# Linformer attention into a maxout block: batch 0 with fewer TensorE instructions, and 120 small products ahead of everything

## The chip, the cores and the metric

The kernel runs on one core of one Trainium2 chip. The metric is device time in microseconds of one execution. Three executions of the kernel before took 319.89, 320.08 and 320.24 us; the median is 320.08 us. Engine names are those of the profile: PE is TensorE (PEld its weight loads), DVE is VectorE, ACT is ScalarE, POOL is GpSimd and SP is SyncE.

## The reference: what is computed

There are 8 batches of 8 heads, 1024 positions and 64 features per head. Keys and values are first projected along the sequence to 64 rows by two constant matrices E and F; then comes ordinary softmax attention; then a feed-forward block whose gate is the larger of two linear maps.

```python
k_proj = np.einsum('ks,bhsd->bhkd', E, k)          # 64 rows instead of 1024
v_proj = np.einsum('ks,bhsd->bhkd', F, v)
scores = scale * np.matmul(q, k_proj.transpose(0, 1, 3, 2))
attn = softmax(scores)                              # over the 64 projected keys
x = np.matmul(attn, v_proj)                         # heads side by side: (8192, 512)
out = np.maximum(x @ w1, x @ w2) @ w_out            # 512 -> 1024 -> 512
```

The inputs are float32 and so is the output; most products run in half precision, with sums in float32.

## The kernel before, in words

**Order.** The order of all instructions is written out by hand: each engine's queue gets its instructions in the order in which the Python code issues them. A long list of slots sets the order from batch 1 on; batch 0 is a straight list of calls (lines 955 to 1004), and it is the only part that the change touches. A "unit" is half of a batch's positions; from batch 1 on, the attention of one unit is woven between the feed-forward products of the unit before.

**Loads.** SP loads E, the first two heads of k (in float32, as `kf_sb`) and F. GpSimd's queue loads the rest with a cast to half precision, in this order: heads 2 and 3 of k, heads 0 to 3 of q, heads 4 to 7 of k, heads 4 to 7 of q (lines 116 to 118), the four pairs of heads of v (L108, called from line 123), then pieces of the weights w2 and w1 (L130, L139), then w_out and the later batches. A weight load is issued when one of eight earlier loads has landed.

**Batch 0.** `step_eft` (L167) transposes E, and later F, in float32 on PE, eight products of 64 columns each; DVE (for E) or ACT (for F) copies the result to half precision as `eft` (L173). `step_kv` (L195) projects k or v: for "k" it makes eight products of 64 output rows and 256 columns for four heads, and DVE copies the result to `kp` (L205). For "v" it works on two heads at a time and makes every product twice, once into the upper and once into the lower 64 rows of the bank (16 products of 128 columns per pair of heads), because the later steps want v in both halves. `step_kpt` (L285) transposes the projected keys, head by head and twice per head, again to have them in both halves of the partitions; DVE copies them to `kpt` (L290). `step_qt` (L311) transposes the queries; DVE copies them to `qt` (L316). `step_sc` (L340 through `score`) makes the scores of four heads and 256 positions: 32 keys at a time, so 16 products on array tiles of 64 rows by 32 columns; ACT takes the exp (L380). `step_dn` (L352) sums the exps by products with ones, on 64x32 tiles, and ACT takes the logarithm (L388); `step_inv` (L427) turns that into the inverse. `step_at` (L352) makes the values, and DVE scales them into `xt` (L443). Then the difference of the weights `wd` is formed by DVE (L540) and the up-projection starts (`up_slots`, L524).

**Dummies.** `warm(n)` (L153) issues n products of 128x512 ones whose result nobody reads. Eight stand in front of all; five, three, and several times two stand between the steps of batch 0.

**PSUM.** Four single banks go round in turn (`mm_bank`), and two double banks (`att_banks`). A step that takes a bank waits until the last reader of the step before it in that bank is done.

**Guard.** Near the end a flag decides whether a second, general version of the kernel (`tile_shifted`) has to run; here it does not. The last product (L1196) waits for a store, so that a fetch of instructions comes behind it.

Of the kernel before, what the change touches and what calls it, by code (L numbers as in the profile page):

```python
# [19 lines left out]
def kernel(  # L20
# [58 lines left out]
    def big(n, dtype=FP16):  # L79
        return const.tile([128, 16384 // mybir.dt.size(dtype) // 2], dtype, tag=f"big{n}", name=f"big{n}")  # L80
# [47 lines left out]
    for g in range(2):  # L128
        for w_sb, w in ((w2_sb, moe_w2), (w1_sb, moe_w1)):
            nc.gpsimd.dma_start(  # L130
                out=w_sb.rearrange("p (g z) f -> p g z f", z=2)[:, g, :, 0:256],
                in_=w.rearrange("(g p z) f -> p g z f", p=128, z=2)[:, g, :, 0:256],
            )
    for w_sb, w, f0, f1 in (
# [3 lines left out]
        for z in range(2):  # L138
            nc.gpsimd.dma_start(  # L139
                out=w_sb.rearrange("p (g z) f -> p g z f", z=2)[:, :, z, f0:f1],  # L140
                in_=w.rearrange("(g p z) f -> p g z f", p=128, z=2)[:, :, z, f0:f1],
# [3 lines left out]
    ones16 = const.tile([128, 512], FP16)  # L145
# [1 line left out]
    junk = const.tile([1, 1], FP16)  # L147


    def warm(n, att=False):  # L150
        w_ps = att_banks()[:, 0, :] if att else mm_bank()
        for _ in range(n):
            nc.tensor.matmul(  # L153
                out=w_ps, lhsT=ones16[:, 0:128], rhs=ones16, start=True, stop=True
            )

    warm(8)
    ident16 = const.tile([128, 128], FP16)
    nc.vector.tensor_copy(out=ident16, in_=ident)


    eft = [const.tile([128, NC, KP], FP16, tag=f"eft{i}", name=f"eft{i}") for i in range(2)]

    def step_eft(i):
        eft_ps = mm_bank()
        for c in range(NC):
            nc.tensor.transpose(  # L167
                out=eft_ps[:, c * KP : (c + 1) * KP],
                in_=ef_sb[:, i].rearrange("k (p c) -> k c p", c=NC)[:, c, :],
                identity=ident[:KP, :KP],  # L170
            )
        eng = nc.scalar.copy if i else nc.vector.tensor_copy
        eng(out=eft[i].rearrange("p c k -> p (c k)"), in_=eft_ps)  # L173


    def new_attn(t):
# [6 lines left out]
    def step_kv(t, h0=0, h1=H, which="kv", att=False, dma=False, copy=nc.vector.tensor_copy, between=None):  # L183
        kv_ps = att_banks()[:, 0, :] if att else mm_bank(n=0 if dma else None)
        n = (h1 - h0) * D
        both = which == "v"
        nh = 2 if both else h1 - h0
        for h in range(0, h1 - h0, nh):
            if h and between is not None:
                between()  # L190
            for c in range(NC):
                for w in which:
                    i = "kv".index(w)
                    for r in range(2) if both else (i,):
                        nc.tensor.matmul(  # L195
                            out=kv_ps[r * KP : (r + 1) * KP, h * D : (h + nh) * D],
                            lhsT=eft[i][:, c, :],
                            rhs=t[w][:, h0 + h : h0 + h + nh, c, :],
                            start=(c == 0), stop=(c == NC - 1),
                        )  # L200
        zd = lambda ap: ap.rearrange("p (h d z) -> p h z d", d=D // 2, z=2)
        if "k" in which:
            eng = nc.vector.tensor_copy if which == "k" or dma else nc.scalar.copy
            kp = t["kp"][:, h0:h1]
            eng(out=kp[:, :, 0, :], in_=kv_ps[0:KP, 0:n].rearrange("p (h d) -> p h d", d=D))  # L205
        if both:
            copy(out=t["vp"][:, h0:h1], in_=zd(kv_ps[:, 0:n]))
        elif "v" in which:
            def finish_v():
                nc.vector.tensor_copy(out=t["vp"][KP:128, h0:h1], in_=zd(kv_ps[KP:128, 0:n]))  # L210
                if dma:
                    nc.vector.tensor_copy(out=kp[:, :, 1, :], in_=kp[:, :, 0, :])
                    step_kpt_dma(t)
                else:
                    step_vp(t, h0, h1)

            if att:
                return finish_v
            finish_v()
# [47 lines left out]

    def kpt_of(t, head, o):
        rows = t["kpt"][o * D : (o + 1) * D]
        if "sets" not in t:  # L270
            return rows[:, head]
        s, m = divmod(head, H // 2)
        return rows[:, 2 * ORDER.index((m - o) % (H // 2)) + s]
# [6 lines left out]

    def step_kpt(t, h0=0, h1=H, att=False):
        kpt_ps = att_banks(FP16)[:, 0, :] if att else mm_bank(FP16)
        for h in range(h0, h1):
            for r in range(2):
                nc.tensor.transpose(  # L285
                    out=kpt_ps[r * D : (r + 1) * D, (h - h0) * KP : (h - h0 + 1) * KP],
                    in_=t["kp"][:, h, 0, :],
                    identity=ident16[:KP, :KP],
                )
        nc.vector.tensor_copy(  # L290
            out=t["kpt"][:, h0:h1, :].rearrange("q h k -> q (h k)"),
            in_=kpt_ps[:, 0 : (h1 - h0) * KP],
        )


    def step_kpt_dma(t):
        nc.sync.dma_start_transpose(
            out=t["kpt"], in_=t["kp"].rearrange("p h r d -> p (h r d)")
        )
# [6 lines left out]
    def step_qt(t, h0, nh=2, i0=0, i1=NI, att=False):  # L306
        qt_ps = att_banks(FP16)[:, 0, :] if att else mm_bank(FP16)
        ni = i1 - i0
        for h in range(nh):
            for i in range(ni):  # L310
                nc.tensor.transpose(  # L311
                    out=qt_ps[:, (h * ni + i) * 128 : (h * ni + i + 1) * 128],
                    in_=t["q"][:, h0 + h, 2 * (i0 + i) : 2 * (i0 + i) + 2, :],
                    identity=ident16,
                )
# [14 lines left out]
    W = HALF // 2  # L330
    Z = D // 2

    def score(t, g, j, banks):
        for h in range(2):
            for o in range(2):
                for e in range(2):
                    head = 4 * g + 2 * h + e
                    for s in range(2):
                        pos = D * (o ^ e) + s * Z
                        nc.tensor.matmul(  # L340
                            out=banks[e][pos : pos + Z, h * W : (h + 1) * W],
                            lhsT=kpt_of(t, head, o)[:, s * Z : (s + 1) * Z],
                            rhs=t["qt"][o * D : (o + 1) * D, head, j * W : (j + 1) * W],
                            start=True, stop=True,
                        )
        t["ex", g, j] = soft.tile([128, 2, HALF], FP16, tag="soft", name="ex_sb")
# [608 lines left out]
    t = tiles[0]  # L955
# [2 lines left out]
    step_eft(0)  # L958
    nc.vector.tensor_copy(out=t["k"][:, 0], in_=kf_sb[:, 0])
    nc.scalar.copy(out=t["k"][:, 1], in_=kf_sb[:, 1])  # L960
    warm(5)
    step_kv(t, 0, 4, "k")
    step_eft(1)
    step_kpt(t, 0, 4)
    warm(3)
    step_qt(t, 0, 4, 0, NI // 2)
    step_qt(t, 0, 4, NI // 2, NI)
    warm(2)
    step_sc(t, 0, 0)
    step_sc(t, 0, 1)  # L970
    warm(2)
    step_kv(t, 4, 8, "k")
    step_dn(t, 0, 0)
    warm(2)
    step_kpt(t, 4, 8)
    step_dn(t, 0, 1)
    step_inv(t, 0, 0)
    step_inv(t, 0, 1)
    warm(2)
    step_qt(t, 4, 4, 0, NI // 2)  # L980
    step_qt(t, 4, 4, NI // 2, NI)
    warm(2)
    step_sc(t, 1, 0)
    step_kv(t, 0, 2, "v")
    step_kv(t, 2, 4, "v")
# [95 lines left out]
    t = tiles[1]  # L1081
# [29 lines left out]
    t = tiles[2]  # L1111
# [8 lines left out]
    for b in range(3, B):  # L1120
        t = tiles[b]
        n = 2 * b - 3
# [13 lines left out]
    for i, (new, old) in enumerate(zip([*groups[1:], none], groups)):  # L1136
        n, h = divmod(i + 2, 2)
# [9 lines left out]
    for n, (b, o) in enumerate(units):  # L1147
# [44 lines left out]
    for reg in regs:  # L1192
# [4 lines left out]
        out=mm_bank()[0:1, 0:1], lhsT=ones16[:, 0:1], rhs=ones16[:, 0:1], start=True, stop=True  # L1197
# [166 lines left out]
```

## Time and profile before

| | |
|---|---|
| median of three executions | 320.08 us |
| span of the profiled execution, first to last instruction | 318.1 us |
| time of the profiled execution beside its span | not listed apart; the median is 2.0 us over the span |
| PE busy | 312.3 us, 98% |
| DVE, ACT, POOL busy | 76%, 65%, 13% |
| PE instructions recorded | 3922 weight loads and 3922 products |
| fetches of instructions on queue q8 | 31 packets, 0.51 MB |
| granted clock of PE | 1.000 over the span |

A line of the lists names the line of the code, the engine, the operation, output and inputs with the buffer numbers left out, shapes, count, and either busy time and mean or start and length; what stands in square brackets is the idle time before it and what ended it. A busy PE is not a PE at its peak, as the ends of products are modelled. In the DMA part, a queue's line gives packets, MB and the time of its packets as a share of the 16 engines' time. q0 holds GpSimd's loads, q1 those of SP and ACT, and q8 fetches instructions in packets of 16 KB.

### The profile page before, as it was taken

How to read it: one execution, taken by the hardware profiler on the slowest of the kernel's cores; microseconds unless marked ns; L12 is line 12 of the kernel's file. 1: busy time of each engine (PE TensorE's matmuls, PEld its weight loads, DVE VectorE, ACT ScalarE, POOL GpSimd, SP SyncE). 2: the span in 40 equal slices, each digit the busy share in tenths (PEclk: the TensorE clock that was granted, in tenths of full speed). 3: DMA queues.
4: the chain of work that ended last, by engine and by line, in shares of the span. 5: the costliest groups of instructions: out<-in, count | busy, mean ns of one | idle time of the engine just before them, and what ended most of it. 6: DMA issues, size and time to landing. Idle time of an engine off the chain costs nothing.

```text
span 318.1 us, 9308 instructions
## 1 busy us (share of the span) xinstructions
PE 312.3 (98%) x3922; PEld 253.6 (80%) x3922; DVE 241.1 (76%) x441; ACT 206.2 (65%) x373; POOL 40.8 (13%) x63
## 2 busy tenths in 40 slices
PE   8989999999999999999999999999999999999996
PEld 3555588888887888788887888788887888888885
DVE  2366888877969696996969696996969696969883
ACT  2476842777776777477776778477776777765541
POOL 8259002003000300022000400030000000000000
PEclk9999999999999999999999999999999999999999
DMA  7999999999979999899999999989979131313124
GB/s 189 206 200 195 207 206 202 207 158 160 204 139 195 162 212 245 210 182 154 223 233 217 167 204 245 215 151 183 232 149 209 45 102 36 102 35 102 36 99 136
DMA packets 76684, 53.71 MB, mean 169 GB/s; under 512 B 29664, under 2 KB 76128, under 8 KB 76640
## 3 DMA queue, kind: packets, MB, share of 16 engines
q0 software_dynamic: 30688, 28.05, 56.0%
q1 hardware_dynamic: 45664, 24.85, 32.7%
q8 instruction: 31, 0.51, 0.6%
q10 hardware_dynamic: 288, 0.20, 0.2%
q14 instruction: 13, 0.11, 0.1%
HBM read 57.15 MB, written 16.78 MB: 232 GB/s over the span
## 4 chain that ended last, share of the span: by engine, by line
PE 92%; DMA 5%; POOL 1%; ACT 1%; issue 0%; DVE 0%; POOLq 0%
PE mm_ps L837 47%; PE mm_ps L745 27%; PE mm_ps L524 4%; DMA v_sb<-in_v_dram 4%; PE att_ps L352 3%; PE mm_ps L195 3%; PE mm_ps L340 2%; PE mm_ps L633 2%; PE att_ps L237 1%; DMA out_dram<-o_sb 1%; PE mm_ps L311 1%; POOL k_sb L108 0%; POOL q_sb L108 0%; ACT ld_sb L388 0%; ACT ex_sb L380 0%
## 5 line engine op out<-in xcount | busy, mean ns | idle before, releaser
L719 ACT COPY p_sb<-mm_ps 128x512 f32<-128x512 f32 x179 | 101.8, 592 | 49.1 <-PE mm_ps L745 27.2
L837 PEld LDWEIGHTS <-big 128*128 128x128 f16 x768 | 73.5, 98 | 11.8 <-issue 3.6
L837 PE MATMUL mm_ps<-T_sb,big 128*128 128x256 f16 x576 | 76.9, 273 | 0.0
L760 DVE TENSOR_TENSOR gt_sb<-mm_ps,p_sb 128x512 f16<-128x512 f32 x56 | 38.5, 687 | 43.0 <-PE mm_ps L745 41.6
L745 PE MATMUL mm_ps<-big,big 128*128 128x256 f16 x336 | 50.4, 273 | 0.0
L745 PEld LDWEIGHTS <-big 128*128 128x128 f16 x448 | 43.8, 98 | 5.1
L837 PE MATMUL mm_ps<-wo_sb,gt_sb 128*128 128x256 f16 x256 | 42.6, 273 | 0.0
L837 PEld LDWEIGHTS <-gt_sb 128*128 128x128 f16 x376 | 35.7, 98 | 6.7 <-issue 2.7
L469 ACT ACTIVATE ex_sb<-mm_ps 128x512 f16<-128x512 f32 x50 | 27.2, 596 | 18.0 <-PE mm_ps L340 12.3
L745 PEld LDWEIGHTS <-wd_sb 128*128 128x128 f16 x336 | 32.9, 98 | 3.8
L745 PE MATMUL mm_ps<-xt_sb,wd_sb 128*128 128x256 f16 x224 | 32.8, 273 | 0.0
L499 DVE TENSOR_TENSOR xt_sb<-att_ps,ld_sb 128x1024 f16<-128x1024 f32 x26 | 31.7, 1219 | 0.2
L837 PE MATMUL mm_ps<-m_sb,xt_sb 128*128 128x256 f16 x128 | 24.4, 273 | 0.0
L303 POOL COPY junk<-qt_sb 1x1 f16<-1x1 f16 x6 | 2.1, 346 | 172.5 <-DMA qt_sb<-q_sb 172.5
L868 DVE TENSOR_TENSOR o_sb<-mm_ps,p_sb 128x512 f32<-128x512 f32 x32 | 21.9, 683 | 2.8 <-ACT p_sb L897 2.0
L763 DVE TENSOR_SCALAR gt_sb<-gt_sb 128x512 f16<-128x512 f16 (+1 forms) x60 | 20.9, 348 | 2.1
L705 DVE TENSOR_TENSOR big<-gt_sb 128x1024 f16<-128x1024 f16 x32 | 21.8, 683 | 0.0
L837 PE MATMUL mm_ps<-wo_sb,big 128*128 128x256 f16 x128 | 21.5, 273 | 0.0
L806 ACT ACTIVATE gt_sb<-mm_ps 128x512 f16<-128x512 f32 x28 | 16.8, 601 | 5.7 <-PE mm_ps L745 5.7
L837 PE MATMUL mm_ps<-T_sb,gt_sb 128*128 128x256 f16 x120 | 20.3, 273 | 0.0
L837 PEld LDWEIGHTS <-xt_sb 128*128 128x128 f16 x188 | 18.3, 98 | 2.3 <-issue 0.2
L760 DVE TENSOR_TENSOR gt_sb<-p_sb 128x512 f16<-128x512 f32 x28 | 19.1, 682 | 0.6 <-ACT p_sb L719 0.6
(121 smaller groups left out, 434.7 us busy)
## 6 DMA issues: line engine op xcount, KB each, us to landing
out_dram<-o_sb SPq DMA_DIRECT2D x62, 256.0 KB
k_sb<-in_k_dram POOLq DMA_DIRECT2D x7, 1024.0 KB, 9.8
v_sb<-in_v_dram POOLq DMA_DIRECT2D x7, 1024.0 KB, 15.3
q_sb<-in_q_dram POOLq DMA_DIRECT2D x5, 1024.0 KB, 23.0
q_sb<-in_q_dram POOLq DMA_DIRECT2D x6, 512.0 KB, 15.8
big<-in_moe_w_dram POOLq DMA_DIRECT2D x12, 128.0 KB, 6.3
v_sb<-in_v_dram POOLq DMA_DIRECT2D x4, 256.0 KB, 13.6
wo_sb<-in_moe_w_out_dram POOLq DMA_DIRECT2D x1, 1024.0 KB, 10.4
```

The lines of the kernel that those rows point to most:

```text
L195: nc.tensor.matmul(out=kv_ps[r * KP : (r + 1) * KP, h * D : (h + nh) * D], lhsT=eft[i][:, c, :], rhs=t[w][:, h0 + h : h0 + h + nh, c, :], ...
L469: nc.scalar.activation(out=t["ex", g, j][:, e, :], in_=banks[e], func=ACTF.Exp, scale=scale)
L499: nc.vector.tensor_tensor(out=x_out(t, g, j).rearrange("q z o n -> q o z n"), in0=at_ps.rearrange("q o (z n) -> q o z n", z=2), in1=ld[:, ...
L524: nc.tensor.matmul(out=h_ps, lhsT=wd_sb[:, r, fb * 128 : (fb + 1) * 128], rhs=t["xt"][:, r, :, j * W : (j + 1) * W], start=(r == 0), stop= ...
L705: nc.vector.tensor_tensor(out=S(i), in0=S(0) if x is None else x, in1=y(), op=op)
L719: copy(out=x, in_=bank)
L745: nc.tensor.matmul(out=bank[:, m * W : (m + 1) * W], lhsT=w_[:, n_, (2 * d + m) * 128 : (2 * d + m + 1) * 128], rhs=a[:, n_, :], start=(n ...
L760: nc.vector.tensor_tensor(out=c_blk(j, c), in0=two(x), in1=two(y), op=ALU.add)
L763: nc.vector.tensor_scalar_max(ap, ap, 0.0)
L806: nc.scalar.activation(out=out, in_=in_, func=ACTF.Relu)
L837: nc.tensor.matmul(out=bank[i][:, 0:CH] if two_banks else bank[:, i * CH : (i + 1) * CH], lhsT=a(c)[:, i * 128 : (i + 1) * 128], rhs=w_(c) ...
L868: nc.vector.tensor_tensor(out=o_sb, in0=two(x), in1=two(y), op=ALU.add)
```

## The change

All of it concerns batch 0 and the start.

- Ahead of everything stands `burst(120)`: 120 products of 64 rows by 32 output columns, 128 columns wide, whose places go round over eight tiles of the array. Behind it stand four dummies instead of eight.
- The dummies inside batch 0 become `warm32`: float32 products with the identity, in blocks of up to four times 128 columns. `warm32(5)` is two instructions, the others one.
- When F is transposed, ACT makes a second copy, `f_twice`, in which each block of F^T stands twice side by side (in the space of `big(3)`, which the transposed weights use later). The v projection of batch 0 uses it as a weight of 128 columns: one product where there were two.
- The keys of batch 0 are copied flat, with the first head repeated behind the last by a small ACT copy; `step_kpt` then transposes two neighbouring heads in one product: four per call instead of eight. `kpt_of` looks up the head accordingly.
- The scores of batch 0 use all 64 keys of a head at once: 8 products on 64x64 tiles instead of 16 on 64x32.

PE's program grows by 60 instructions in all: 240 come in front and 180 go from batch 0.

```diff
-    def warm(n, att=False):
-        w_ps = att_banks()[:, 0, :] if att else mm_bank()
+    def warm(n):
+        w_ps = mm_bank()
...
-    warm(8)
+    def warm32(n):
+        w_ps = mm_bank()
+        for i in range(0, n, 4):
+            m = min(4, n - i)
+            nc.tensor.matmul(
+                out=w_ps[:, 0 : m * 128], lhsT=ident,
+                rhs=ident[:, None, :].broadcast_to([128, m, 128]), start=True, stop=True,
+            )
+
+    def burst(n):
+        w_ps = att_banks()
+        for i in range(n):
+            a, z = divmod(i % 8, 4)
+            nc.tensor.matmul(
+                out=w_ps[32 * z : 32 * z + 32, a, 0:128],
+                lhsT=ones16[64 * a : 64 * a + 64, 0:32],
+                rhs=ones16[64 * a : 64 * a + 64, 0:128],
+                start=True, stop=True,
+            )
+
+    burst(120)
+    warm(4)
...
+    f_twice = big(3)[:, 0 : NC * 2 * KP].rearrange("p (c k) -> p c k", c=NC)
...
+        if i:
+            nc.scalar.copy(
+                out=f_twice.rearrange("p c (r k) -> p c r k", r=2),
+                in_=eft_ps.rearrange("p (c k) -> p c k", k=KP)[:, :, None, :].broadcast_to([128, NC, 2, KP]),
+            )
...
-                    for r in range(2) if both else (i,):
-                        nc.tensor.matmul(
-                            out=kv_ps[r * KP : (r + 1) * KP, h * D : (h + nh) * D],
-                            lhsT=eft[i][:, c, :],
...
+                    nc.tensor.matmul(
+                        out=kv_ps[:, h * D : (h + nh) * D] if both
+                        else kv_ps[i * KP : (i + 1) * KP, h * D : (h + nh) * D],
+                        lhsT=f_twice[:, c, :] if both else eft[i][:, c, :],
...
+            if which == "k":
+                flat = kp.rearrange("p h r d -> p (h r d)")
+                eng(out=flat[:, 0:n], in_=kv_ps[0:KP, 0:n])
+                nc.scalar.copy(out=flat[:, n : n + D], in_=kv_ps[0:KP, 0:D])
...
-        for h in range(h0, h1):
-            for r in range(2):
-                nc.tensor.transpose(
-                    out=kpt_ps[r * D : (r + 1) * D, (h - h0) * KP : (h - h0 + 1) * KP],
-                    in_=t["kp"][:, h, 0, :],
...
+        flat = t["kp"][:, h0:h1].rearrange("p h r d -> p (h r d)")
+        for h in range(h1 - h0):
+            nc.tensor.transpose(
+                out=kpt_ps[:, h * KP : (h + 1) * KP],
+                in_=flat[:, h * D : (h + 2) * D],
...
-                    for s in range(2):
-                        pos = D * (o ^ e) + s * Z
+                    z = D if t is tiles[0] else Z
+                    for s in range(0, D, z):
+                        pos = D * (o ^ e) + s
...
-    warm(5)
+    warm32(5)
```

The other calls of `warm` inside batch 0 become calls of `warm32` with the same argument.

More of the change, by code (lines that the diff above doesn't have):

```diff
@@ L193, in step_kv @@
                     i = "kv".index(w)
-                    for r in range(2) if both else (i,):
-                        nc.tensor.matmul(
-                            out=kv_ps[r * KP : (r + 1) * KP, h * D : (h + nh) * D],
-                            lhsT=eft[i][:, c, :],
-                            rhs=t[w][:, h0 + h : h0 + h + nh, c, :],
-                            start=(c == 0), stop=(c == NC - 1),
-                        )
+                    nc.tensor.matmul(
+                        out=kv_ps[:, h * D : (h + nh) * D] if both
+                        else kv_ps[i * KP : (i + 1) * KP, h * D : (h + nh) * D],
+                        lhsT=f_twice[:, c, :] if both else eft[i][:, c, :],
+                        rhs=t[w][:, h0 + h : h0 + h + nh, c, :],
+                        start=(c == 0), stop=(c == NC - 1),
+                    )
         zd = lambda ap: ap.rearrange("p (h d z) -> p h z d", d=D // 2, z=2)
@@ L204, in step_kv @@
             kp = t["kp"][:, h0:h1]
-            eng(out=kp[:, :, 0, :], in_=kv_ps[0:KP, 0:n].rearrange("p (h d) -> p h d", d=D))
+            if which == "k":
+                flat = kp.rearrange("p h r d -> p (h r d)")
+                eng(out=flat[:, 0:n], in_=kv_ps[0:KP, 0:n])
+                nc.scalar.copy(out=flat[:, n : n + D], in_=kv_ps[0:KP, 0:D])
+            else:
+                eng(out=kp[:, :, 0, :], in_=kv_ps[0:KP, 0:n].rearrange("p (h d) -> p h d", d=D))
         if both:
@@ L269, in kpt_of @@
         rows = t["kpt"][o * D : (o + 1) * D]
+        if t is tiles[0]:
+            n = H // 2
+            return rows[:, head // n * n + (head - o) % n]
         if "sets" not in t:
@@ L282, in step_kpt @@
         kpt_ps = att_banks(FP16)[:, 0, :] if att else mm_bank(FP16)
-        for h in range(h0, h1):
-            for r in range(2):
-                nc.tensor.transpose(
-                    out=kpt_ps[r * D : (r + 1) * D, (h - h0) * KP : (h - h0 + 1) * KP],
-                    in_=t["kp"][:, h, 0, :],
-                    identity=ident16[:KP, :KP],
-                )
+        flat = t["kp"][:, h0:h1].rearrange("p h r d -> p (h r d)")
[3 more added lines that the diff above has]
+                in_=flat[:, h * D : (h + 2) * D],
+                identity=ident16[:KP, :KP],
+            )
         nc.vector.tensor_copy(
@@ L337, in score @@
                     head = 4 * g + 2 * h + e
-                    for s in range(2):
-                        pos = D * (o ^ e) + s * Z
+                    z = D if t is tiles[0] else Z
+                    for s in range(0, D, z):
+                        pos = D * (o ^ e) + s
                         nc.tensor.matmul(
-                            out=banks[e][pos : pos + Z, h * W : (h + 1) * W],
-                            lhsT=kpt_of(t, head, o)[:, s * Z : (s + 1) * Z],
+                            out=banks[e][pos : pos + z, h * W : (h + 1) * W],
+                            lhsT=kpt_of(t, head, o)[:, s : s + z],
                             rhs=t["qt"][o * D : (o + 1) * D, head, j * W : (j + 1) * W],
@@ L964 @@
     step_kpt(t, 0, 4)
-    warm(3)
+    warm32(3)
     step_qt(t, 0, 4, 0, NI // 2)
     step_qt(t, 0, 4, NI // 2, NI)
-    warm(2)
+    warm32(2)
     step_sc(t, 0, 0)
     step_sc(t, 0, 1)
-    warm(2)
+    warm32(2)
     step_kv(t, 4, 8, "k")
     step_dn(t, 0, 0)
-    warm(2)
+    warm32(2)
     step_kpt(t, 4, 8)
@@ L978 @@
     step_inv(t, 0, 1)
-    warm(2)
+    warm32(2)
     step_qt(t, 4, 4, 0, NI // 2)
     step_qt(t, 4, 4, NI // 2, NI)
-    warm(2)
+    warm32(2)
     step_sc(t, 1, 0)
```

## The prediction

> **What bounds the kernel now.** I read the page first (busy time), then PE's waits, the chain of waits from 17 to 28 us, the time-ordered list of the first 32 us, and last the DMA queues in narrow stretches.
>
> ```profile
> span 318.1 us, 9308 instructions
> PE 312.3 (98%) x3922; PEld 253.6 (80%) x3922; DVE 241.1 (76%) x441; ACT 206.2 (65%) x373; POOL 40.8 (13%) x63
> ```
>
> The list of PE's waits over the whole span (total us, times, longest):
>
> ```profile
> PE mm_ps L195 <- DMA v_sb<-in_v_dram: 0.5, 2, 0.3
> PE att_ps L352 <- ACT vp_sb L207: 0.5, 1, 0.5
> ```
>
> TensorE is full from about 23 us to the end; its only waits inside the work lie in batch 0. The change touches nothing behind batch 0 on the path, so its time is the shift of the moment at which PE becomes continuous. The chain of waits there (start, length):
>
> ```profile
> 5.54 13.33 DMA v_sb<-in_v_dram
> ...
> 18.92 0.64 PE mm_ps L195 x16
> 19.56 0.28 PE att_ps L352 x8
> ...
> 19.86 0.60 ACT ld_sb L388
> 20.46 0.91 ACT ex_sb L380
> ...
> 22.39 0.33 ACT vp_sb L207
> ...
> 22.76 0.63 PE att_ps L352 x32
> 23.39 1.83 PE mm_ps L524 x8
> ```
>
> The second v pair lands at 18.88; then the sums (L352), then ScalarE without a pause from 19.86 to 22.72, then values, then the up-projection (L524). Beside it runs a VectorE chain and a load gate (list in order of time):
>
> ```profile
> 20.49 2.48 DVE L443 TENSOR_TENSOR xt_sb<-mm_ps,ld_sb 128x512 f16<-128x512 f32 x4 [0.60 <-ACT ld_sb L388]
> 22.89 0.48 DVE L540 TENSOR_TENSOR wd_sb<-big,big 128x256 f16<-128x256 f16 x2
> 27.02 0.69 DVE L540 TENSOR_TENSOR wd_sb<-big,big 128x1024 f16<-128x1024 f16 x1 [0.89 <-DMA big<-in_moe_w_dram]
> 27.77 3.13 PEld L524 LDWEIGHTS <-wd_sb 128*128 128x128 f16 x16 [0.42 <-DVE wd_sb L540]
> ```
>
> So two chains meet at 23.3 to 23.4 (ScalarE's, and VectorE's 20.49 + 2.48 + 0.48), and at 27.7 PE is held once more by a weight load through VectorE (27.02 + 0.69 = 27.71). A gain ahead of 27 us is worth only what this gate gives back too.
>
> Why v lands when it does. GpSimd issues each weight load on the landing of an earlier one, so its idle ends show landings; and a narrow stretch of the DMA queues shows the fetch of PE's instructions (q8: packets, MB, share):
>
> ```profile
> 13.11 0.70 POOL L130 DMA_DIRECT2D big<-in_moe_w_dram x1 [1.81 <-DMA k_sb<-in_k_dram]
> 15.65 0.71 POOL L130 DMA_DIRECT2D big<-in_moe_w_dram x1 [1.84 <-DMA q_sb<-in_q_dram]
> 18.27 0.70 POOL L139 DMA_DIRECT2D big<-in_moe_w_dram x1 [1.92 <-DMA v_sb<-in_v_dram]
> ```
>
> ```profile
> q8 instruction: 31, 0.51, 0.6%
> ```
>
> From 15.9 to 16.0 us, and from 22.9 to 23.0 us:
>
> ```profile
> q8 instruction: 1, 0.02, 59.1%
> q8 instruction: 1, 0.02, 58.4%
> ```
>
> 1 MB of q takes 15.65 - 13.11 = 2.54 us, so half of it, the first v pair, should take 1.27 us and end GpSimd's wait at 16.9; it ends at 18.27, 1.35 us late. In that stretch lies one 16 KB fetch of instructions. A fetch sits on one DMA engine and holds that engine's sixteenth of every load behind it. 7,844 recorded PE instructions over 31 fetches is one per 253. Counted in the code, the 256th instruction is the second key transpose (15.0 us), the 512th lies in the values L352 at 20 us: the fetches show 0.9 and about 3 us later.
>
> **The change, part by part.** PE in the front and ScalarE, from the same list:
>
> ```profile
> 1.47 3.59 PE L153 MATMUL mm_ps<-ones 128*128 128x512 f16 x8 [1.47 <-DVE ones L146]
> 4.99 1.09 PE L167 MATMUL mm_ps<-ident,big 64*128 64x64 f32 x8
> 6.02 1.25 PE L153 MATMUL mm_ps<-ones 128*128 128x512 f16 x5
> 7.29 1.06 PE L195 MATMUL mm_ps<-k_sb,eft 128*64 128x256 f16 x8
> 10.36 1.07 PE L311 MATMUL mm_ps<-ident,q_sb 128*128 128x128 f16 x16
> 17.34 0.41 PE L340 MATMUL att_ps<-qt_sb,kpt_sb 64*32 64x256 f16 x16
> 18.03 0.64 PE L195 MATMUL mm_ps<-v_sb,eft 128*64 128x128 f16 x16 [0.28 <-DMA v_sb<-in_v_dram]
> 19.61 0.40 PE L340 MATMUL att_ps<-qt_sb,kpt_sb 64*32 64x256 f16 x16
> ```
>
> ```profile
> 9.42 0.59 ACT L173 CAST eft<-mm_ps 128x512 f16<-128x512 f32 x1 [2.25 <-PE mm_ps L167]
> 12.27 1.94 ACT L380 ACTIVATE ex_sb<-att_ps 128x1024 f16<-128x1024 f32 x2 [2.27 <-PE att_ps L340]
> 17.82 1.02 ACT L380 ACTIVATE ex_sb<-att_ps 128x1024 f16<-128x1024 f32 x1 [0.57 <-PE att_ps L340]
> 25.71 1.01 ACT L562 COPY big<-att_ps 128x1024 f16<-128x1024 f16 x1 [2.47 <-PE att_ps L556]
> ```
>
> *Burst and four dummies for eight.* Eight dummies take 3.59 us, about 0.43 each, where five later ones take 1.25, 0.25 each: PE starts at half rate and is at full rate by 6 us. Four fewer give back 1.7 us. The burst spreads over eight array tiles, as the scores do. Sixteen score products of 256 columns take 0.41 with the pipeline's end; 120 of 128 columns at half rate are 7.5 such groups of equal time, at most 3.1 us, and 1.6 us if groups of eight follow each 0.107 us (half of the 256-column step, 0.43 / 2 / 2). I take 1.6 to 2.2, nearest to the scores' own overlap: 0 to 0.5 us later at 4.99.
>
> *fp32 dummies.* The eight fp32 transposes of 64 columns take 1.09, about 0.11 each behind the first, four times a half-precision 64-column pass (16 transposes of 128 columns in 1.07: 0.06 each). So 640 fp32 columns cost what 5 x 512 half-precision ones did, 1.1 us; I take 0 for all, with up to 0.05 per call for the wider weight load, 0.35 over seven calls.
>
> *Full key transposes, doubled F for v.* Products halve, but two half-width products ran side by side before: 16 in 0.64 us become 8 of the same 128 columns, 0.45 + the end. 0 on the path, bounds -0.2 to +0.1. The transposes: 0 to +0.1 each.
>
> *Extra ScalarE work.* The doubled copy (1024 wide; 1.01 us by L562) follows the eft copy: 10.0 to 11.0. ScalarE's next work is at 12.27, so 1.2 us of cover. But the second query transposes reuse that bank and now wait for it: 11.1 instead of 10.8, hidden behind VectorE's first query copy and the first exp. The two wrap copies (64 wide) are under 0.3 each; the second stands ahead of the first Ln, worth 0 to 0.1.
>
> *64x64 scores.* Eight products in two rounds instead of sixteen in two: no time saved. But the tile shape changes between the sums (64x32), the scores and the values. Its price between shapes, from batch 1:
>
> ```profile
> 59.41 0.60 PE L837 MATMUL mm_ps<-wo_sb,gt_sb 128*128 128x256 f16 x4
> 59.94 0.41 PE L352 MATMUL mm_ps<-ex_sb,vp_sb 64*32 64x256 f16 x16
> ```
>
> Four products at 0.11 end at 59.85; the smaller tiles start at 59.94: 0.09. The second score step of group 1 (19.61) gets two such changes, up to 0.2, ahead of the values and so of VectorE's chain at 20.49. The Trainium skill (TensorEngine Tiling (Array Packing), Key Properties) says that a change of tiling mode, not merely of tile, drains the engine; by that rule this part costs instead of saving, and the 0.09 us agree with it.
>
> *The fetches.* The burst's 240 instructions put the 256th into the first transposes at 5 us (the sequencer runs ahead, so the fetch can start from 3 us on, and by 8 us at the latest with the lag seen), and the 512th into the v pairs at 18.9. So one DMA engine is about 1.2 us late for the rest of k, F and q already, and v is no earlier than before: the same engine still carries the same 16 KB ahead of it. The k product then starts at about 7.9 instead of 7.29, F's transposes at 9.1 instead of 8.3, the queries at 11.1 instead of 10.36, and with the doubled copy and the small terms the score step of 17.34 comes 0.7 to 1.0 later. Its exp ended at 18.84; the sums started at 19.48 (19.56 - 0.08), so 0.64 us of this is cover. What is left is 0.1 to 0.4 us; with the tile changes the VectorE chain is 0.2 to 0.6 late at 23.3; the gate at 27.77 swallows what PE waits there now: at most the 0.42 of its row, likely near 0.1, as products of 0.23 each (1.83 / 8) were still running ahead of it. Net: **+0.3 us**. Bounds: -0.2 with a free fetch and +0.9 with every term at its upper end (both below).
>
> The sum stands against the profiled execution: span 318.1; the timed median is 320.08, 2.0 us more, which I leave untouched: 320.08 + 0.3 = **320.4 us**. 0.2% of it, 0.64 us, is about what a measurement of this kernel can tell from no change.
>
> The Trainium skill (Runtime: NRT & Kernel Launch, Instruction fetch mechanics) says instructions come in 16 KiB blocks of 256, fetched by the sequencer's own DMA queue and mostly hidden. The size agrees (0.51 MB over 31); "hidden" does not, since the v load is 1.35 us late beside one.
>
> **The rivals.**
> *The early fetch is free* (0.15). If DMA engines have room before 6 us, the first v pair lands at 16.9 and the second about 0.9 earlier. The sums are then held by the exp to 19.0, 0.45 earlier; but the second fetch, now near 19 us, still delays another engine's share of the weights, so the gate moves by 0.2 only. -0.2 us, 319.9. Only if the second fetch too misses the weights is it -0.8, 319.3 (0.07 on top). Against: the landings follow each other without a gap (2.54 us per MB), so an engine once late has no room to catch up, and before 6 us the same engines carry E, F and k.
> *The front runs out of cover* (0.25): slower. A burst that PE can only issue slowly (3.1 us), late F and q, and wider fp32 weight loads add up on one chain; from 0.64 us of lateness at the score step each further 0.1 costs 0.1. At 1.6 late: +0.9, 321.0.
> *The burst does not raise the clock* (0.11). If small tiles count little as load, full rate comes one warm-up later (3.5 us, 1.47 to 5.0): transposes, dummies and the k product (about 3 us of work) take twice as long. +2.5 less 0.64 and 0.1 of cover: +1.7, 321.8. For it: half rate is seen until the first eight are through. Against: PE is as continuously busy as before. The doubled rows would show it at 5 to 8 us.
>
> **How the numbers follow.** My forecast, -0.1 to +0.6 us, has 0.42; free fetch 0.22 (0.15 and 0.07), no cover 0.25, clock 0.11. Faster by 0.2%: 0.07. Slower: 0.36, of which 0.25 and 0.11. Same: 0.57. The range drops the clock case and most of the -0.8 case: 319.6 to 321.3; the likeliest case's own is 320.0 to 320.7.
>
> **What would show it.** After: a q8 packet between 3 and 8 us, none near 16; GpSimd's wait that ends at 13.11 and 15.65 now later by about 1; the v waits at 18.0 to 18.9 as before; scores at 18.0 to 18.4; L524 first at 23.4 to 23.9; the burst 1.6 to 2.2 us long. Wrong if k and q land as before (then -0.2), or if L167 and the dummies at 5 to 8 us run at half rate.

## The result, and the profile after

The changed kernel took 321.22 us (median of five executions, 320.76 to 321.66) against 320.08: ratio 1.0037, 95% interval 1.0026 to 1.0048. It is slower by 1.14 us, where the forecast was slower by 0.3 with a range up to 321.3. Measured again beside other kernels it took 321.47 us (six executions), ratio 1.0053, interval 1.0034 to 1.0071.

The page of the profiled execution, span and busy time:

```profile
span 319.4 us, 9395 instructions
PE 312.5 (98%) x3964; PEld 255.7 (80%) x3964; DVE 241.9 (76%) x441; ACT 207.2 (65%) x376; POOL 40.3 (13%) x63
```

PE does the same 312 us of work and the span is 1.3 us longer, so the time went into waiting. (1.3 and not 1.14, as the profiled execution of the kernel before is one of its shorter ones: in the later runs an execution's time is 1.8 us over its own span, so it took about 319.9.) The page records 42 products more than before (3964 against 3922), so 84 instructions of PE with the weight loads and not the 60 of the description; a float32 dummy stands in it as two. PE's waits (total us, times, longest; left out are those for the ones at the start, for the last store and for the second exp, which the kernel before has too):

```profile
PE mm_ps L190 <- DMA big<-in_F_dram: 1.1, 1, 1.1
PE mm_ps L222 <- DMA k_sb<-in_k_dram: 0.5, 1, 0.5
PE att_ps L389 <- ACT vp_sb L240: 0.5, 1, 0.5
PE mm_ps L347 <- ACT big L198: 0.2, 1, 0.2
```

The two waits for v are gone and a wait for F is there. The DMA queues from 6.9 to 7.0 us show what F has in its way (packets, MB, share), and there is no such packet from 15.9 to 16.0 us, where the kernel before had one:

```profile
q8 instruction: 1, 0.02, 64.4%
```

PE's front in order of time (start, length; wait before in brackets):

```profile
1.47 1.80 PE L170 MATMUL att_ps<-ones 64*32 64x128 f16 x120 [1.47 <-DVE ones L146]
...
5.04 1.08 PE L190 MATMUL mm_ps<-ident,big 64*128 64x64 f32 x8
6.04 1.35 PE L161 MATMUL mm_ps<-ident 128*128 128x512 f32 x4
...
7.88 1.03 PE L222 MATMUL mm_ps<-k_sb,eft 128*64 128x256 f16 x8 [0.49 <-DMA k_sb<-in_k_dram]
...
9.99 1.07 PE L190 MATMUL mm_ps<-ident,big 64*128 64x64 f32 x8 [1.07 <-DMA big<-in_F_dram]
...
12.64 0.61 PE L347 MATMUL mm_ps<-ident,q_sb 128*128 128x128 f16 x8 [0.18 <-ACT big L198]
...
16.23 0.70 PE L161 MATMUL mm_ps<-ident 128*128 128x256 f32 x2
...
19.32 0.41 PE L377 MATMUL att_ps<-qt_sb,kpt_sb 64*64 64x256 f16 x8
```

The rows of the kernel before that these are compared with:

```profile
8.30 1.08 PE L167 MATMUL mm_ps<-ident,big 64*128 64x64 f32 x8
...
19.49 0.30 PE L352 MATMUL att_ps<-ex_sb,ones 64*32 64x256 f16 x8
...
23.32 1.90 PE L524 MATMUL mm_ps<-xt_sb,wd_sb 128*128 128x512 f16 x8
```

And the chain of waits, which before ran through the v load (5.54, 13.33 us long) and now runs through F:

```profile
2.03 7.82 DMA big<-in_F_dram
...
9.99 1.08 PE mm_ps L190 x8
...
11.09 0.58 ACT eft L196
11.68 0.92 ACT big L198
...
12.64 0.61 PE mm_ps L347 x8
...
19.39 0.37 PE att_ps L377 x8
...
19.78 1.03 ACT ex_sb L417
...
20.86 0.35 PE att_ps L389 x8
...
24.11 0.63 PE att_ps L389 x32
24.74 1.90 PE mm_ps L561 x8
```

How the shift travels: F's transposes start 1.69 us later (9.99 against 8.30), the score step 1.98 (19.32 against 17.34), the sums behind it 1.37 (20.86 against 19.49), the up-projection 1.42 (24.74 against 23.32), and the span ends 1.3 later. By the landing events in the trace, fifteen sixteenths of F are there at 8.64 and the last one at 9.86. The first half of q has the same gap: 10.45 and 11.69.

### The profile page after: what moved, and what is told of

It reads as the page before. It is cut to its first block, busy times and chain, and to the rows that moved or that the text cites. A ratio compares the mean times of both kernels' runs of the same rounds, so it can differ in the third digit from the quotient of the medians.

```text
span 319.4 us, 9395 instructions
## 1 busy us (share of the span) xinstructions
PE 312.5 (98%) x3964; PEld 255.7 (80%) x3964; DVE 241.9 (76%) x441; ACT 207.2 (65%) x376; POOL 40.3 (13%) x63
## 4 chain that ended last, share of the span: by engine, by line
PE 94%; DMA 3%; ACT 2%; SPq 0%; issue 0%; DVE 0%
PE mm_ps L874 47%; PE mm_ps L782 27%; PE mm_ps L561 4%; PE att_ps L389 4%; PE mm_ps L222 3%; PE mm_ps L377 2%; DMA big<-in_F_dram 2%; PE mm_ps L670 2%; PE att_ps L270 1%; PE mm_ps L347 1%; PE mm_ps L161 1%; DMA out_dram<-o_sb 1%; ACT ex_sb L417 1%; PE att_ps L377 1%; ACT ld_sb L425 0%; PE mm_ps L190 0%
## 5 line engine op out<-in xcount | busy, mean ns | idle before, releaser
L874 PEld LDWEIGHTS <-big 128*128 128x128 f16 x768 | 73.5, 98 | 11.8 <-issue 3.6
L506 ACT ACTIVATE ex_sb<-mm_ps 128x512 f16<-128x512 f32 x50 | 27.2, 597 | 18.0 <-PE mm_ps L377 12.3
L800 DVE TENSOR_SCALAR gt_sb<-gt_sb 128x512 f16<-128x512 f16 (+1 forms) x60 | 21.8, 364 | 2.1
L339 POOL COPY junk<-qt_sb 1x1 f16<-1x1 f16 x6 | 1.1, 177 | 173.3 <-DMA qt_sb<-q_sb 173.3
```

Of the source, the lines that this page charges most:

```text
L506: nc.scalar.activation(out=t["ex", g, j][:, e, :], in_=banks[e], func=ACTF.Exp, scale=scale)
L800: nc.vector.tensor_scalar_max(ap, ap, 0.0)
L874: nc.tensor.matmul(out=bank[i][:, 0:CH] if two_banks else bank[:, i * CH : (i + 1) * CH], lhsT=a(c)[:, i * 128 : (i + 1) * 128], rhs=w_(c) ...
```

## The experiments

Twelve kernels ran. The kernel before was timed beside each: 320.06, 320.09, 320.12 and 319.94 us in the four comparisons, 92 executions, of which two were above 320.81 us.

**The burst alone (e1).** The kernel before with only the burst:

```diff
-    warm(8)
+    burst(120)
+    warm(4)
```

> The kernel before with the burst of 120 products and four dummies in place of the eight dummies, nothing else changed. Early fetch (theory): the 256th PE instruction comes in the first transposes again, a q8 packet shows between 5 and 8 us, F's transposes start near 9.9 instead of 8.30, the queries near 11.7, and the first L524 comes 0.6 to 1.0 us later than before's 23.32; time 320.6 to 321.1. Rival, the edits inside batch 0 are what costs: no edit is here, so F's transposes at 8.3 to 8.5, first L524 at 23.3 to 23.5, time 320.0 to 320.3. Rival, the burst itself is slow or leaves the clock low: the burst took 1.80 us in the changed kernel and the transposes ran at full rate, so 0 to 0.1.

Measured 321.82 us, ratio 1.0039 (1.0024 to 1.0054): as much as the whole change, and above the 320.6 to 321.1 that was expected. The six executions fall into two kinds. Two, with a granted clock of 1.0, took 320.56 and 320.62; four, with 0.993 to 0.995, took 321.78 to 322.26. The profiled one is of the second kind. Its clock in three stretches (stretch; length; busy us of PE, PEld, DVE, ACT, POOL, with their counts; granted clock; DMA share and GB/s):

```profile
8.80:12.20 3.40, 2.04 (x20) 1.41 (x21) 0.60 (x2) 0.58 (x1) 0.00 (x0) 1.00 1.23 205
12.20:15.60 3.40, 3.40 (x51) 2.27 (x50) 1.38 (x2) 0.07 (x1) 1.36 (x2) 0.50 1.24 206
15.60:19.00 3.40, 3.40 (x55) 1.69 (x40) 0.71 (x2) 2.80 (x4) 0.94 (x3) 1.00 1.25 207
```

and its F transposes:

```profile
10.16 1.07 PE L179 MATMUL mm_ps<-ident,big 64*128 64x64 f32 x8 [1.51 <-DMA big<-in_F_dram]
...
12.17 1.88 PE L323 MATMUL mm_ps<-ident,q_sb 128*128 128x128 f16 x16
```

The waits for late loads left PE busy for 2.04 of 3.40 us, and in the next 3.40 us it ran at half clock: the queries took 1.88 us for 1.07. So the early fetch has a price of its own, some 0.5 us, and in some executions a second one through the clock.

**No burst, and half a burst (e2, e3).** The changed kernel with eight dummies in front, and with 60 products and six dummies:

```diff
-    burst(120)
-    warm(4)
+    warm(8)
```

> The changed kernel with the eight dummies of before in place of the burst: the edits inside batch 0 alone. Early fetch (theory): no q8 packet before 14 us, F's transposes at 8.3 to 8.6, queries at 10.4 to 10.8, first L524 at 23.0 to 23.6, time 319.8 to 320.3. Rival, the edits inside batch 0 cost: score step of 17.34 at 18.3 or later and first L524 at 24.3 or later as in the changed kernel, time 320.8 to 321.3.

> The changed kernel with a burst of 60 products and six dummies: the 256th PE instruction moves to the first scores, so the first fetch should show between 10 and 15 us. Early fetch (theory): E, F and the first q load land as before (F's transposes 8.3 to 8.6, queries 10.4 to 10.8); only the later k and q loads and v are late by 1.0 to 1.3 us; time between the two, 320.0 to 320.6. Rival, edits inside batch 0: 320.8 to 321.3, as with 120.

Measured 320.16 us (ratio 1.0015, 1.0002 to 1.0027) and 320.78 (1.0027, 1.0015 to 1.0039). In the profiled executions the first fetch lies at 16.41 and 13.20 us, behind F; F's transposes start at 8.77 and 8.75, and the score step at 18.13 and 18.16. So without the early fetch about 1.0 us of the loss goes. In e3 the loads ahead of its fetch have no late sixteenth (F whole at 8.61, the first half of q at 10.61), and the next load to land behind it has one: fifteen sixteenths of the second half of q at 15.66, the last at 16.63. The late sixteenth goes with the fetch, not with the burst. Again there are two kinds: e2 has eight executions at 319.98 to 320.23 and four at 320.90 to 321.62, e3 seven at 320.08 to 320.80 and four at 321.62 to 321.71. All show a clock of 1.0, which counts only from the first record of the clock in an execution. The median of e3, above the 320.0 to 320.6 expected, is therefore no size of anything.

**F later in the order (e7).** If F's late sixteenth is the cause, its steps can go behind the second k product:

```diff
     step_kv(t, 0, 4, "k")
-    step_eft(1)
     step_kpt(t, 0, 4)
...
     step_kv(t, 4, 8, "k")
+    step_eft(1)
```

> The changed kernel with F's transposes and both their copies moved behind the second k product (the wait for F, 1.07 us, and the wait for the doubled copy leave the chain of the first scores; the fetch stays early). Early fetch (theory): first queries wait for their load at 11.7 alone, the first scores come 0.5 to 0.9 earlier than 13.67, the score step of 19.32 at 18.4 to 18.9; time 0.4 to 0.9 below the changed kernel: 320.3 to 320.8. Rival, the slower float dummies and smaller edits alone make it late: less than 0.3 us gained, 320.9 to 321.3.

A miss: 322.62 us, ratio 1.0084 (1.0063 to 1.0105), slower by 1.4 than the changed kernel. The front of its profiled execution:

```profile
6.09 2.50 PE L161 MATMUL mm_ps<-ident 128*128 128x512 f32 x4
8.52 1.75 PE L222 MATMUL mm_ps<-k_sb,eft 128*64 128x256 f16 x8
```

The dummies took 2.50 us for 1.35 and the k product 1.75 for 1.03: PE was at half rate until 10.0 us, where the clock's first record stands (5.5 in the kernel before). The reorder itself did not pay either. The first scores start at 13.38, 0.29 us earlier than in the changed kernel in spite of the late clock, but the score step of 19.32 comes at 20.20, where 18.4 to 18.9 was expected: F's transposes now stand at 15.86 between the second k product and the sums and take 1.02 us of PE's time there, which the expectation had not counted. Three of the six executions also show a clock of 0.995 or less. The run raised the question of what makes the clock rise.

**Which part makes the second kind (e9, e8, e5, e6).** e9 is the kernel before with float32 dummies alone; e8 is the changed kernel without burst and with half-precision dummies; e5 keeps the burst and takes half-precision dummies; e6 takes back the 64x64 scores.

```diff
-    warm(5)
+    warm32(5)
...
-    warm(2)
+    warm32(2)
```

> The kernel before with one edit of the change alone: its 18 dummies behind the first eight become float32 products of 512 columns at most, 9 instructions' worth of calls, 8 for 18. The program is otherwise the kernel before, so the first instruction fetch falls near 16 us as there and the loads are not touched. Theory A (all of the loss is the early fetch that delays one DMA engine's share of F, the queries and the keys): 320.0 to 320.3, and all runs lie together as those of the kernel before do (319.55 to 320.62). Theory B (float32 dummies weigh less for the clock that TensorE is granted, or end less evenly, so that in some runs the clock in front comes later or falls back): the median may stay at 320.1, but some runs lie 1.3 to 1.6 us above the others, as in the run without the burst (320.0 to 320.2 and 320.9 to 321.6). By the forecast's own bound for the seven calls (0 to 0.35 us) the most that the products themselves can cost is 0.35.

> The changed kernel with neither the 120 small products nor the float32 dummies: eight dummies of half precision in front and half-precision dummies behind them, as in the kernel before; the full key transposes, the 64x64 score tiles and the doubled F^T for v stay. Theory A (early fetch alone): 320.0 to 320.3, as the run without the burst in its lower group. Theory B (float32 dummies make the second group): 319.9 to 320.2 with no run above 320.7. If neither (the spread comes from the doubled copy or from key transposes and scores in fewer instructions): two groups again, 1.3 to 1.6 us apart. The first fetch should fall between 13 and 18 us.

> The changed kernel with its burst, but with half-precision dummies in place of the float32 ones. The burst still moves the first instruction fetch to about 7 us, so F's last sixteenth lands at 9.7 to 10.0 us and the score step starts at 19.0 to 19.5. Theory A (early fetch): as long as the changed kernel, 321.0 to 321.4. Theory B (float32 dummies weigh on the clock): 320.6 to 321.0, less a part of the loss, as the clock is less often late. The front is then between 0 and 0.35 us shorter by the dummies' own time.

```diff
-                    z = D if t is tiles[0] else Z
+                    z = Z
```

> The changed kernel with one edit undone: batch 0's scores in tiles of 64x32 as before, two instructions for one. Both theories (early fetch; float32 dummies): 321.0 to 321.4, as the changed kernel, since neither has to do with the scores. The forecast's bound for the 64x64 tiles was a cost of up to 0.2 us for changes of tile shape: were they that, this run is 0.2 shorter; if fewer instructions save time on the path, it is up to 0.2 longer. Sixteen and eight instructions more in front of the end of the score steps move the later fetches by as much, without effect.

e9: 320.30 us, ratio 1.001 (0.999 to 1.0031), eight executions at 319.92 to 320.56 and four at 321.49 to 321.69. e8: 320.09, ratio 0.9996 (0.9978 to 1.0013), all twelve at 319.90 to 320.59. So the second kind comes with the float32 dummies, and the edits of batch 0's own steps (keys, scores, doubled F) cost nothing together that can be seen. e8's front:

```profile
8.69 1.09 PE L189 MATMUL mm_ps<-ident,big 64*128 64x64 f32 x8
...
17.72 0.41 PE L376 MATMUL att_ps<-qt_sb,kpt_sb 64*64 64x256 f16 x8
...
23.41 1.90 PE L560 MATMUL mm_ps<-xt_sb,wd_sb 128*128 128x512 f16 x8
```

From F's transposes to the score step it takes 9.03 us, the kernel before 9.04 (17.34 - 8.30).

e5: 320.64, ratio 1.0016 (0.9996 to 1.0035); one execution of 1128 us stands apart (the median of the other eleven is 320.62), nine lie at 320.48 to 320.94 and two at 321.40 and 321.71. That is theory B's range. This is the early fetch with little else, +0.55 us; the interval reaches just below no change, but it agrees with the two executions of e1 at full clock (0.50 and 0.56 above 320.06):

```profile
9.64 1.06 PE L190 MATMUL mm_ps<-ident,big 64*128 64x64 f32 x8 [0.93 <-DMA big<-in_F_dram]
...
18.64 0.41 PE L377 MATMUL att_ps<-qt_sb,kpt_sb 64*64 64x256 f16 x8
...
24.05 1.90 PE L561 MATMUL mm_ps<-xt_sb,wd_sb 128*128 128x512 f16 x8
```

Again 9.00 us from F's transposes to the score step; the changed kernel needs 9.33. That is the float32 dummies' own time: one of 256 columns takes 0.65 to 0.70 us where two half-precision ones took 0.59 to 0.61.

e6: 321.57 us, ratio 1.0038 (1.002 to 1.0057), four of twelve at a clock of 0.995. It lies beside the changed kernel (321.22 and 321.47), a little above the 321.0 to 321.4 expected, so the tile size decides little; 0.2 us could not be told in executions that spread from 320.81 to 322.26.

**Which float32 call (f1, f2).** The kernel before, with only the call at 6 us in float32, and with all calls but that one:

```diff
-    warm(5)
+    warm32(5)
```

> The kernel before with only its first call of dummies behind the eight, the one at 5.9 us, in float32; the other 13 dummies stay half precision. Theory R (at that place the clock is not yet full; where float32 dummies stand there, it rises about 3.4 us later in some runs, the recorded clock of 1.0 in the long runs counting only from its rise): two groups, 3 to 5 of 12 at 321.4 to 321.8, the others at 319.9 to 320.4. Theory S (the calls behind F's transposes thin the work out later): one group at 319.9 to 320.4.

> The kernel before with all calls of dummies but the first in float32: the first call at 5.9 us stays half precision. Theory R: one group at 319.9 to 320.4, and a rise of the clock between 4 and 6 us. Theory S: two groups, 3 to 5 of 12 at 321.4 to 321.8.

f1: 320.15 us, ratio 1.0011 (1.0001 to 1.0021), seven of eleven at 319.95 to 320.39 and four at 320.82 to 321.44, a little less far off than expected. f2: 320.08, ratio 1.0001 (0.9992 to 1.001), all eleven at 319.91 to 320.73. Taken together: with the call at 6 us in float32 and no early fetch (e2, e3, e9, f1), 16 of 46 executions lie above 320.81; with half precision there (before, e8, f2), 2 of 115. The line is drawn close, as e3 has one at 320.80 and f1 one at 320.82; above 321.2 it is 12 of 46 against 1 of 115. The six later calls are the ones that lengthen the path (f2):

```profile
8.91 1.07 PE L176 MATMUL mm_ps<-ident,big 64*128 64x64 f32 x8
...
18.19 0.41 PE L349 MATMUL att_ps<-qt_sb,kpt_sb 64*32 64x256 f16 x16
...
23.59 1.90 PE L533 MATMUL mm_ps<-xt_sb,wd_sb 128*128 128x512 f16 x8
```

9.28 us from F's transposes to the score step, 0.24 more than before. In this execution F came late too, so the score step is 0.85 late; the cover ahead of the sums takes up 0.58 of that; the up-projection is 0.27 late, and that shows in the span (318.4 against 318.1). Over the eleven executions the median is no longer than the kernel before's.

**The changed kernel once more (f3).**

> The changed kernel itself again, beside these. If the early fetch (0.5 us by the run with the burst and half-precision dummies) and the second group (4 of 12 runs 1.5 us longer) simply add up: about two thirds of its runs at 320.5 to 321.2 and one third at 321.5 to 322.3, and a median of 320.8 to 321.3. If they hinder each other (the late loads leave TensorE idle where the clock is decided): more than half above 321.4.

321.47 us; one of six lies below 321.2 and three above 321.4. Neither case came as written: more than a third are long, and no more than half, so the two prices do not simply add. This profiled execution has its clock's first record at 9.6 us:

```profile
6.09 2.50 PE L161 MATMUL mm_ps<-ident 128*128 128x512 f32 x4
8.59 1.53 PE L222 MATMUL mm_ps<-k_sb,eft 128*64 128x256 f16 x8
10.05 1.09 PE L190 MATMUL mm_ps<-ident,big 64*128 64x64 f32 x8
```

So the late rise happens in the changed kernel itself. It costs little there (F's transposes at 10.05 for 9.99), since PE would have waited for F anyway. Two sixteenths of the first two heads of k also landed late in this execution, at 7.56 and 7.90, so the k product could not have started much before 8.5 at any clock.

**No dummies at 6 us (g1).** The kernel before without that call:

```diff
-    warm(5)
```

> The kernel before without its five dummies at 6.0 us; all else as there, the first fetch near 16 us. TensorE is then idle between E's transposes (end 6.0) and the first k product (7.3). Theory R (what TensorE does between 5.9 and 7.2 us decides whether the clock is full then or 3.4 to 5 us later): the first rise of the clock lies at 8 to 12 us in the profile, the k product takes about 1.75 us for 1.06, and most runs are 321.2 to 321.8, where the long runs of the float32 dummies lie. Rival (the long runs have another cause): 319.7 to 320.3, with the rise between 4 and 6 us as before.

321.65 us, ratio 1.0061 (1.0043 to 1.008); all six at 320.76 to 322.98, two of them in the 321.2 to 321.8 that theory R expected. What PE does at this place matters, but the profiled execution (320.81) does not show the late rise of theory R. The clock rose at 5.5 us, and fell again:

```profile
5.50:8.90 3.40, 1.64 (x15) 1.33 (x14) 1.12 (x2) 0.62 (x1) 2.90 (x5) 1.00 1.22 240
8.90:12.30 3.40, 3.40 (x27) 2.40 (x28) 0.71 (x2) 0.59 (x1) 0.71 (x1) 0.50 1.24 205
12.30:15.70 3.40, 3.24 (x55) 1.86 (x52) 1.29 (x2) 1.89 (x2) 0.70 (x1) 0.99 1.25 207
```

PE was busy for 1.64 of 3.40 us and then had half the clock for 3.40. Two executions of 321.63 and 321.67 with a clock of 1.0 may be of the other sort, as long as the long ones of e9; neither was profiled.

Traces with the early fetch show how little work is too little. The emptiest stretch of the changed kernel, that of e5, and that of e6 with the stretch behind it:

```profile
8.88:12.29 3.41, 2.34 (x23) 1.92 (x23) 0.71 (x2) 1.40 (x3) 0.32 (x1) 1.00 1.24 207
8.17:11.58 3.41, 2.48 (x21) 1.59 (x20) 0.71 (x2) 1.05 (x3) 0.36 (x1) 1.00 1.24 203
8.39:11.80 3.41, 2.14 (x19) 1.66 (x19) 0.71 (x2) 1.17 (x3) 0.03 (x1) 1.00 1.23 205
11.80:15.21 3.41, 3.41 (x50) 2.23 (x47) 1.38 (x2) 0.76 (x2) 1.38 (x2) 0.50 1.23 204
```

The changed kernel and e5 kept the clock behind these stretches; e6 lost it, as e1 and g1 did behind 2.04 and 1.64 us of work.

**F in all traces.** F is whole at 9.50 to 10.03 us in the six profiled executions with the early fetch, and at 8.16 to 8.77 in the eight without. The kernel before has the earliest of all.

No version came out below the kernel before: e8 and f2 equal it.

## Why the prediction was right, and where it was not

The direction, the rival and the range held; the size did not. The case that came is the rival "The front runs out of cover", priced at +0.9 with a chance of 0.25; two of its three parts came (late F, float32 dummies), the slow burst did not. That the range held is narrow and in part luck: 321.22 lies 0.08 us under its top, and the second measurement, 321.47, above it.

- *What held.* The fetch moved to 6.94 us, one DMA engine is 1.2 us late (F 9.86 against 8.64, q 11.69 against 10.45), and v's second pair is no earlier (19.35 against 18.88). The burst took 1.80 us (forecast 1.6 to 2.2), E's transposes start at 5.04 (4.99 plus 0 to 0.5), the k product at 7.88 (7.9). The cover is 0.61 us (1.98 - 1.37; 0.64). The gate gave back 0.1 (1.42 - 1.3; "likely near 0.1"); in e8 and f2, whose up-projections start 0.09 and 0.27 later and whose spans are 0.1 and 0.3 longer, it gave back nothing that can be seen.
- *Signs that failed with the size.* The scores came at 19.32 (18.0 to 18.4), the first up-projection at 24.74 (23.4 to 23.9), and the waits for v are gone, because PE came later than v.
- *The step that failed: "F's transposes at 9.1 instead of 8.3".* They start at 9.99. The 9.1 is about where the late k product ends (7.9 and its 1.06), so F was given no delay of its own. It had no slack: its last sixteenth came at 8.16, and the transposes start 0.14 later at 8.30, as they do in the changed kernel (9.86, 9.99). With the 1.2 us that the prediction had worked out for the engine, F ends at 9.4 and its transposes stand at 9.5; e5 has 9.64. The rest of the way to 9.99 is that E and F came 0.5 later in this execution, apart from the late sixteenth (half of E's sixteenths by 4.54, 4.04 in the kernel before; 3.96 to 4.54 over the profiled executions, with no order by kernel).
- *The term that was mis-sized: "I take 0 for all" of the float32 dummies.* They cost 0.29 on the path (9.33 against 9.04), near the upper end that I gave, 0.35. Alone this costs no time in the median (f2); behind a late F it does.
- So "the score step of 17.34 comes 0.7 to 1.0 later" was 1.98: 1.69 from F and 0.29 from the dummies. Both draw on one cover of 0.61: e5 spends it on F and pays 0.55, and there each further term is paid in full. With the dummies that is about 0.85 of the 1.14. In the first profile the rest is the later start of the loads, in f3's profile it is the k product, which ends only at 10.05; what it is in the medians of five and six executions is not shown.
- *The rest of batch 0.* Costed at nothing, and e8 bears it out. The doubled copy holds PE for 0.18 us ahead of the second queries (forecast 0.3 later, hidden); it stands on the chain of waits, so it is not hidden, but e8 has the same wait (0.27) and needs no more time in all. In the changed kernel the scores stand 0.23 us behind the sums' start and the values 0.34 behind the scores' (21.09 - 20.86, 21.43 - 21.09), where the kernel before had 0.12 and 0.21: 0.24 for two changes of tile, just over the forecast's 0.2. With the small tiles back, e6 has 0.11 and 0.21 again. It is nearly hidden: from the sums to the up-projection the changed kernel takes 3.88 us (24.74 - 20.86), the kernel before 3.83 and e6 3.81. The Trainium skill (TensorEngine Tiling (Array Packing), Key Properties) names such a drain; these rows agree with it.
- *The rival "The burst does not raise the clock"* did not come as written. The burst can raise it: the clock is up by 4.8 us in e5 and by 5.5 in the changed kernel's first profile. Without the full burst, the executions that are longer at a clock of 1.0 come with the float32 call at 6 us; with it, e7 and f3 show a late rise. Its price can be estimated from e7: the k product is through at 10.27 (8.52 and 1.75), 1.36 us later than in the changed kernel's first profile (7.88 and 1.03). Where F is in time and the cover is spent this is all paid, and the long executions of e9 lie 1.4 to 1.6 above the middle of the others (320.13).

What stays open: none of the long executions of e2, e3, e9 or f1 was the profiled one, so that they are late rises is argued from f1, f2, g1 and from the traces of f3 and e7, not shown. Why float32 products that keep PE busy as long (1.35 us for 1.25) count for less is not settled either. In e7 and f3 they may not be the cause: if the clock's stretches of 3.41 us run back from the rises at 9.98 and 9.65, the rise that failed to come was due at 6.57 and 6.24, with PE busy without a gap in the stretch before and no more than 0.5 us of the float32 call in it. So there the burst, or E's transposes at 5.02, may be what counts for less; that with the burst and half precision (e1, e5) only one execution of 17 is long at a clock of 1.0 (321.40, e5) speaks for the float32 call again, but does not settle it. Nor was it tried whether the load start of 3.96 to 4.54 us depends on the kernel.

## What to carry to other kernels

Instructions put in front of everything move every later fetch of instructions: count where the next multiples of 256 fall (one fetch per 253 recorded instructions in the kernel before), and look at which load is in flight there, for one DMA engine's sixteenth of it will be late by the fetch (here 1.0 to 1.5 us). When several small delays meet the same slack, add them up first and subtract the slack once; and carry a load's delay to each reader through that reader's own slack. Dummies that keep the clock up are part of the timing: change their kind or place only with many executions at hand, since the harm showed in a third of them here.

## What the runs showed of the hardware

- PE's clock changes in stretches of 3.4 us. Half-rate stretches lay at 8.9 to 12.3 (g1), 12.2 to 15.6 (e1) and 11.8 to 15.2 us (e6); the ones ahead of them had PE busy for 1.64, 2.04 and 2.14 of 3.4 us, while 2.34 (the changed kernel) and 2.48 (e5) kept the clock. The Trainium skill (TensorE: Matmul & The Clock Gate, Part 1: The HAM clock gate) has a free-running window of about 3.4 us; the traces agree on the length, and on the start, which differs from execution to execution. That a window filled to 0.63 with work (2.14 of 3.41) already loses the clock, and one filled to 0.69 keeps it, is these five traces' own number. For the rise it does not suffice: PE was busy throughout where e7's and f3's clock stayed down.
- A late rise leaves the recorded mean clock at 1.0, since the records begin with the rise: the length of known products (2.50 for 1.35 us) shows it.
- A fetch of 16 KB at 7 us delays one sixteenth of every load behind it, without recovery: F by 1.2 us, and the first quarter of v still by 1.27 (18.11 against 16.84 for the other fifteen). That it is one DMA engine's share is read from the sixteenths; the trace does not name the engine.
